# Regrouping the attention matmuls in a fused attention and bilinear kernel

## The chip, the cores and the metric

The kernel runs on one core of one Trainium2 chip. Its metric is the device time of one execution in microseconds (us), and lower is better. The core has a matmul engine (PE, with its weight loads shown as PEld), a vector engine (DVE), a scalar engine (ACT), a third engine for elementwise work (POOL), and a queue engine (SP) that issues nearly all transfers between memory and the core.

## The reference

Attention inside chunks of 64 tokens, for 8 batches of 576 tokens and 8 heads of size 64, is followed by a bilinear feed-forward layer over all 4608 tokens:

```python
q_c = q.reshape(B, H, nc, chunk, D)          # the same for k and v; chunk = 64
scores = scale * np.matmul(q_c, k_c.transpose(0, 1, 2, 4, 3))
scores = scores - np.max(scores, axis=-1, keepdims=True)
attn = np.exp(scores)
attn = attn / (np.sum(attn, axis=-1, keepdims=True) + 1e-09)
out = np.matmul(attn, v_c)                   # back to (B, H, S, D)

x = out.transpose(0, 2, 1, 3).reshape(B * S, H * D)     # 4608 x 512
a = x @ w_a                                  # 512 x 1536
b = x @ w_b
y = a * b @ w_out                            # 1536 x 512
```

## The kernel before

**Tiling.** The tokens are cut into 18 units of 256 for the attention, and 9 blocks of 512 (two units each) for the feed-forward part. All instruction orders are written out by hand: nothing reorders instructions within an engine, and each engine runs its own list in order, held up only by what it waits for.

**One unit of attention** has these steps:
- `load` brings q, k and v from memory in float32 on SP's queue. Eight staging buffers (`st`) are shared by all loads.
- `cast` makes bfloat16 copies on POOL (`q_raw`, `k_raw`, `v_raw`; for q and k of unit 0 on DVE).
- q and k are transposed into `qkt`. Units 0 to 4 use PE (`transpose_pe`, L231) with copies out of PSUM by DVE and ACT (L240). From unit 5 on, SP issues two DMA transposes per unit (`transpose_dma`, L245), which wait for the casts.
- `scores` are 64 small matmuls of 64x64 (L265) into two PSUM banks, and then two exponentials on ACT (L276), one for each bank, giving E.
- `sums` multiply E by ones on PE, four 64x64 matmuls of 512 columns (L292), into two banks; ACT takes the logarithm (L302).
- `inverse` is an exponential of minus that logarithm on ACT (L311), either for both halves at once or for one half (`cl`).
- `values` are 64 small matmuls of E with v (L325) into two banks; DVE multiplies each bank by the inverse sums and writes `xT` (L334).

All these matmuls but the transposes use PE as four tiles of 64x64; all others use it whole (128x128).

**The feed-forward part** takes three forms. Block 0 uses whole steps (`ab_step`, L388: a pair of four matmuls for wb and wa; ACT copies one bank out, L396; DVE multiplies, L397). Block 1 does the same in halves of 256 tokens, `h(1)` being one pair for a strip `ft` of 128 columns; there are 24, ft 0 to 11 for each half. From block 2 on, one level of Strassen-like sums is used: `Group` does seven products (`p1` to `p7`, L438) with ACT copies (L449, L456) and DVE sums and products (L476, L477, L488). The output of block 0 is made by `out_part` (L642, three parts of four matmuls for each 128 tokens), and that of later blocks by `OutGroup` (L574) in 14 parts `n0` to `n6`, two each, which a list `chunks` deals out over the Groups of the next block. These parts need sums that POOL makes (`combine_ab` L518, `combine_wo` L164): n3 needs the last `combine_wo`, and n5 the sum `so4`.

**The order around the change.** At the start, PE does transposes of unit 0, q transposes of unit 1, scores of 0, k transposes of 1, sums of 0, two warm-up matmuls, scores of 1, values of 0. In the second half of block 1, attention of units 4 and 5 is strewn between the pairs ft 7 to 11 and the outputs of block 0, with each step of attention on its own. In block 2, `attention` says after which product each step runs; from block 3 on, the scores of the next unit follow the values of the one before directly, through `scores_beside`, with one exponential at once and the other after `p5`.

**PSUM.** There are eight banks: one each in `psum_a`, `psum_c`, `psum_o`, `psum_q`, two buffers in `psum_t` taken in turn, and two pools in the list `psum_b`, which each call of `bank(psum_b)` turns round by one. `bank()` without a pool takes the next of the list `spread`:

```python
        if pool is None:
            pool = spread[0]
            spread.append(spread.pop(0))
        if pool is psum_b:
            pool = psum_b[0]
            psum_b.append(psum_b.pop(0))
```

In block 1 `spread` is `[psum_t, psum_b]`, so that each step of attention takes one bank of either kind. A matmul into a bank waits until the last reader of its earlier content is done.

Of the kernel before, what the change touches and what calls it, by code (L numbers as in the profile page):

```python
# [16 lines left out]
def kernel(  # L17
# [49 lines left out]
    psum_b = [psum_b0, psum_b1]  # L67
    psum_c = ctx.enter_context(tc.tile_pool(name="psumc", bufs=1, space=PSUM))
    psum_o = ctx.enter_context(tc.tile_pool(name="psumo", bufs=1, space=PSUM))
# [27 lines left out]
    def keep_warm(n):  # L97

        t = bank()
        for _ in range(n):  # L100
            nc.tensor.matmul(t, warm_in[:, :128], warm_in, start=True, stop=True)
# [85 lines left out]
    def load(U, names="qkv"):  # L187

        for n in names if U < NU else "":
            src = {"q": q, "k": k, "v": v}[n]  # L190
            if U < PE_UNITS and n != "v":
                st = st_pool.tile([128, H, 2, D], FP32, name="st")
                for r, b, s, m in pieces(U):
                    nc.sync.dma_start(
                        out=st[r // 2:(r + m) // 2].rearrange("p h i d -> p h (i d)"),
                        in_=src[b, :, s:s + m, :].rearrange("h (p i) d -> p h (i d)", i=2),
                    )
                staged[n, U] = st.rearrange("p h i d -> p i h d")
            else:
                staged[n, U] = st_pool.tile([128, 2, H, D], FP32, name="st")  # L200
                load_natural(staged[n, U], src, U)
# [16 lines left out]
    def transpose_pe(U, names="qk"):  # L218
        if U not in qkt:
            qkt[U] = qkt_pool.tile([128, 2, 2, NKT, 128], BF16, name="qkt")  # L220
        for n in names:
            w = "qk".index(n)
            src = raw.pop((n, U))
            t = [bank() for _ in range(2 if U < 2 else 1)]
            tp = [
                t[i % len(t)].bitcast(BF16).rearrange("c (i m p) -> c i m p", i=2, m=NKT)[:, i]
                for i in range(2)
            ]
            for i in range(2):
                for m in range(NKT):  # L230
                    nc.tensor.transpose(  # L231
                        tp[i][:, m, :],
                        src[:, i, 2 * m:2 * m + 2, :].rearrange("p j d -> p (j d)"),
                        identity,
                    )
            dst = qkt[U][:, w].rearrange("c g m (p i) -> c i m g p", i=2)
            for i in range(2):
                on_dve = i == 0 if U == 0 else w == 0 or U == 1
                cp = nc.vector.tensor_copy if on_dve else nc.scalar.copy
                cp(out=dst[:, i], in_=tp[i].rearrange("c m (g p) -> c m g p", g=2))  # L240
# [13 lines left out]

    late = []

    def scores(U, pools=(None, None)):
        t = qkt.pop(U)
        E_of[U] = sm_pool.tile([128, 2, NKT, 2, 64], BF16, name="E")
        sc = [bank(p).rearrange("p (m g s) -> p m g s", m=NKT, g=2) for p in pools]  # L260
        for m in range(NKT):
            for g in range(2):
                for j in range(2):
                    for cl in range(2):
                        nc.tensor.matmul(  # L265
                            sc[j][cl * 64:cl * 64 + 64, m, g, :],
                            t[j * 64:j * 64 + 64, 1, g, m, cl * 64:cl * 64 + 64],
                            t[j * 64:j * 64 + 64, 0, g, m, cl * 64:cl * 64 + 64],
                            start=m == 0 and g == 0,
                            stop=True,  # L270
                            skip_group_check=True,
                        )
        E = E_of[U]
        for j in range(2):
            late.append(
                lambda j=j: nc.scalar.activation(  # L276
                    out=E[:, j], in_=sc[j], func=AF.Exp, scale=scale
                )
            )
        exps(1 if pools[0] else 2)  # L280

    def exps(n=2):
        while late and n:
            late.pop(0)()
            n -= 1

    def sums(U, halves=None):
        E = E_of[U]
        sm = [bank() for _ in range(2)]
        for cl in range(2):  # L290
            for j in range(2):
                nc.tensor.matmul(  # L292
                    sm[cl][j * 64:j * 64 + 64, :],
                    ones[cl * 64:cl * 64 + 64, :],
                    E[cl * 64:cl * 64 + 64, j].rearrange("p m g s -> p (m g s)"),
                    start=True,
                    stop=True,
                )
        ln_of[U] = sm_pool.tile([128, 2, NKT, 128], FP32, name="ln")
        rs_of[U] = ln_of[U]  # L300
        for cl in range(2):
            nc.scalar.activation(  # L302
                out=ln_of[U][:, cl].rearrange("p m n -> p (m n)"), in_=sm[cl], func=AF.Ln
            )
            if halves:
                inverse(U, cl)

    def inverse(U, cl=None):

        for c in [slice(0, 2)] if cl is None else [cl]:  # L310
            nc.scalar.activation(  # L311
                out=rs_of[U][:, c], in_=ln_of[U][:, c], func=AF.Exp, scale=-1.0
            )
# [39 lines left out]
    def bring(U, before_v=()):  # L353

        if U >= NU:
            return
        cast(U, "qk")
        load(U + 1, "q" if U < 8 else "qkv")
        transpose_dma(U)
        for args in before_v:  # L360
            cast(*args)
        bring_v(U)

    def bring_v(U):
        cast(U, "v")
        if U < 8:
            load(U + 1, "kv")

    ab_tiles = {}
# [268 lines left out]
    def out_part(K, tg, part, pool):  # L638
        if part == 0:
            out_ps[K, tg] = bank(pool)  # L640
        for ft in range(4 * part, 4 * part + 4):
            nc.tensor.matmul(  # L642
                out_ps[K, tg],
                ab_tiles[K][:, ft, tg * 128:tg * 128 + 128],
                wo_sb[:, ft],
                start=(ft == 0),
                stop=(ft == NFT - 1),
            )
        if part == 2:
            out_tile(K, tg, out_ps.pop((K, tg)))  # L650

    with tc.manual_schedule(
# [25 lines left out]
        cast_ab(1)  # L678
        cast_ab(2)
        cast_ab(3)  # L680
        transpose_pe(1, "q")
        scores(0)
        transpose_pe(1, "k")
        sums(0, halves=None)
        keep_warm(2)
        scores(1)
        inverse(0)
        values(0)
# [66 lines left out]
        def h(n=1):  # L755
            for _ in range(n):
                half(*halves.pop(0))

        def normalize(U):
            sums(U)  # L760
            inverse(U)

        def out_0(tg):
            for p in range(3):
                out_part(0, tg, p, psum_b)
# [19 lines left out]
        scores(4)  # L785
        out_0(1)
        h(1)
        normalize(4)
        h(1)
        scores(5)  # L790
        cast(7, "q")
        h(1)
        combine_ab(1, 0, 1)
        cast(7, "k")
        load(8, "q")
# [2 lines left out]
        combine_ab(1, 2, 1)  # L798
        bring_v(7)
        values(4)  # L800
        h(1)
        spread[:] = [psum_q, psum_o]
        out_part(0, 2, 0, psum_b)
        normalize(5)
        out_part(0, 2, 1, psum_b)
        out_part(0, 2, 2, psum_b)
        spread[:] = [psum_t]
        values(5)
        h(1)
# [10 lines left out]
        def at(K, i, n, f, u):  # L820
            if u < NU:
                attention.setdefault((K, i, n), []).append(lambda: f(u))

        def scores_beside(pool):
            return lambda u: scores(u, (pool, psum_b[0]))

        for K in range(2, NBLK):
            U = 2 * K + 2
            if K == 2:
                at(K, 0, 0, lambda u: combine_x(2, (2, 3)), U)  # L830
                at(K, 0, 0, scores, U)
                at(K, 0, 1, sums, U)
            else:
                attention[K, 0, 0] = [lambda K=K: combine_x(K, (2,))]
                attention[K, 0, 1] = [lambda K=K: combine_x(K, (3,))]
                at(K, 0, 0, sums, U)
            at(K, 1, 0, inverse, U)
            at(K, 2, 1, values, U)
            at(K, 2, 1, scores_beside(psum_o), U + 1)
            at(K, 3, 0, sums, U + 1)  # L840
            at(K, 3, 1, inverse, U + 1)
            at(K, 4, 1, values, U + 1)
            if K == 2:
                at(K, 5, 1, scores, U + 2)
            else:
                at(K, 4, 1, scores_beside(psum_q), U + 2)
            at(K, 5, 0, lambda u: combine_x(u // 2, (0,)), U + 1)
            at(K, 5, 1, lambda u: combine_x(u // 2, (1,)), U + 1)

        def attend(K, i, n):  # L850
# [2 lines left out]

        last = None
        chunks = {
            2: (1, 1, 1, 1, 1, 2, 1, 2, 1, 1, 2, 1),
            4: (1, 1, 1, 1, 2, 1, 1, 2, 2, 0, 1, 1),
            NBLK - 1: (1,) * 12,
        }
# [8 lines left out]
        for K in range(2, NBLK):  # L868
            for i in range(NWP):
# [16 lines left out]
                now = Group(K, i)  # L886
# [72 lines left out]
```

The softmax here doesn't subtract the row's maximum and nothing guards it: scores larger than these inputs give would overflow.

## Time and profile before

| | |
|---|---|
| median of 7 runs | 304.65 us (303.8 to 305.18) |
| the profiled execution | 303.8 us, of which the span of its instructions is 302.0 |
| PE | busy 289.0 us, 96% of the span |
| DVE, ACT, POOL | busy 208.0, 196.2 and 193.6 us |
| first feed-forward matmul (L388) | 18.61 us |
| first product of block 2 (L438) | 79.46 us |
| first product of block 3 | 110.94 us |
| granted PE clock | full throughout |

All times within the span are counted from its start. A row of the timeline gives start, duration, engine, line, operation, output and inputs, shape and count. A row of the waits gives the total, the number and the longest of them, for one line of an engine and what it waited for. The chain of waits is followed back from the last instruction to what released each step.

### The profile page before, as it was taken

To read this page: it belongs to the slowest core of one execution; us is meant where nothing else is said; L and a number is where in the kernel's file an instruction comes from. 1 tells how busy PE (TensorE), PEld (TensorE's weight loads), DVE (VectorE), ACT (ScalarE), POOL (GpSimd) and SP (SyncE) were. 2 spreads that over 40 slices of the span, in tenths; PEclk is the share of its full clock that TensorE was granted. 3 is DMA by queue.
4 is the path that set the end of the run, shared out by engine and by line. 5 is a ranking of instruction groups with operands and counts; after the bars stand their busy time and mean duration, and the time that the engine had idled before them with its cause. 6 is when DMAs were issued, how large, how long until landed. Compare 5 with 4: busy or idle time off the path is not lost.

```text
span 302.0 us, 8543 instructions
## 1 busy us (share of the span) xinstructions
PE 289.0 (96%) x3497; PEld 231.1 (77%) x3499; DVE 208.0 (69%) x339; ACT 196.2 (65%) x354; POOL 193.6 (64%) x180
## 2 busy tenths in 40 slices
PE   2889999999999999999999999999999999999995
PEld 1434467866587888888888888888888888888884
DVE  3446665865886686769677966796679667965773
ACT  2553567447586668776877687768776876566522
POOL 0666758994999897728880888178817901790660
PEclk9999999999999999999999999999999999999999
DMA  7999999998999999799969585958621001100025
GB/s 229 302 377 285 276 328 361 226 219 191 218 265 227 230 218 255 176 206 226 289 121 216 165 202 112 224 176 192 138 75 72 2 2 69 73 0 3 0 92 188
DMA packets 143079, 54.56 MB, mean 181 GB/s; under 512 B 120256, under 2 KB 137152, under 8 KB 143040
## 3 DMA queue, kind: packets, MB, share of 16 engines
q1 hardware_dynamic: 142896, 53.88, 71.4%
q8 instruction: 27, 0.44, 0.6%
q10 hardware_dynamic: 144, 0.13, 0.1%
q14 instruction: 12, 0.10, 0.1%
HBM read 37.75 MB, written 9.44 MB: 156 GB/s over the span
## 4 chain that ended last, share of the span: by engine, by line
PE 74%; POOL 9%; DMA 8%; SPq 3%; ACT 2%; DVE 2%; issue 2%; POOLq 0%; DVEq 0%; ACTq 0%
PE pb L438 18%; PE pc L438 12%; PE po L574 11%; PE pa L438 11%; PE pq L574 9%; DMA st<-in_q_dram 3%; PE pb L388 3%; DMA st<-in_moe_w_out_dram 3%; SPq L182 2%; POOL so L518 2%; POOL wot L164 2%; DMA st<-in_v_dram 2%; PE pc L388 1%; PE po L388 1%; PE pt L292 1%
## 5 line engine op out<-in xcount | busy, mean ns | idle before, releaser
L518 POOL TENSOR_TENSOR so<-ab_sb 128x512 f16<-128x512 f16 x23 | 27.6, 1198 | 65.9 <-DVE ab_sb L488 65.9
L438 PEld LDWEIGHTS <-t 128*128 128x128 f16 x504 | 48.3, 98 | 8.5 <-issue 1.8
L438 PE MATMUL pb<-s,wa 128*128 128x256 f16 x336 | 50.6, 273 | 0.0
L438 PE MATMUL pa<-xT,wb 128*128 128x256 f16 x336 | 50.4, 273 | 0.0
L476 DVE TENSOR_TENSOR c_sb<-pc,v_sb 128x512 f32<-128x512 f32 x42 | 28.9, 687 | 26.2 <-ACT v_sb L449 26.2
L574 PEld LDWEIGHTS <-ab_sb 128*128 128x128 f16 x384 | 37.6, 98 | 4.7 <-issue 0.4
L438 PEld LDWEIGHTS <-wb 128*128 128x128 f16 x336 | 32.9, 98 | 4.0
L438 PEld LDWEIGHTS <-wa 128*128 128x128 f16 x336 | 31.7, 98 | 4.3 <-issue 0.2
L449 ACT COPY u_sb<-pb 128x512 f32<-128x512 f32 x42 | 24.7, 587 | 15.8 <-PE pb L438 15.6
L488 DVE SCALAR_TENSOR_TENSOR ab_sb<-pc,c_sb 128x512 f16<-128x512 f32 x42 | 29.0, 689 | 7.8 <-PE pc L438 6.3
L488 DVE SCALAR_TENSOR_TENSOR ab_sb<-pb,b_sb 128x512 f16<-128x512 f32 x42 | 29.0, 689 | 6.8 <-PE pb L438 5.9
L574 PEld LDWEIGHTS <-so 128*128 128x128 f16 x288 | 28.1, 98 | 3.6 <-issue 0.3
L456 ACT COPY pb<-pa 128x512 f32<-128x512 f32 x42 | 24.0, 572 | 10.4 <-PE pa L438 10.1
L449 ACT COPY b_sb<-pa 128x512 f32<-128x512 f32 x42 | 25.0, 595 | 8.1 <-PE pa L438 6.9
L477 DVE TENSOR_TENSOR pc<-pc,u_sb 128x512 f32<-128x512 f32 x42 | 28.9, 688 | 0.0
L518 POOL TENSOR_TENSOR so<-so,ab_sb 128x512 f16<-128x512 f16 x23 | 27.0, 1174 | 1.7
L449 ACT COPY v_sb<-pb 128x512 f32<-128x512 f32 x42 | 24.6, 586 | 4.7 <-PE pb L438 3.9
L518 POOL TENSOR_TENSOR ab_sb<-ab_sb 128x512 f16<-128x512 f16 x23 | 26.7, 1162 | 0.0
L518 POOL TENSOR_TENSOR so<-ab_sb,so 128x512 f16<-128x512 f16 x23 | 26.1, 1161 | 0.0
L438 PE MATMUL pb<-s,t 128*128 128x256 f16 x168 | 25.3, 273 | 0.0
L438 PE MATMUL pc<-xT,t 128*128 128x256 f16 x168 | 25.2, 272 | 0.1
L438 PE MATMUL pc<-s,t 128*128 128x256 f16 x168 | 25.2, 273 | 0.0
(133 smaller groups left out, 561.1 us busy)
## 6 DMA issues: line engine op xcount, KB each, us to landing
out_dram<-o_sb SPq DMA_DIRECT2D x34, 256.0 KB, 2.4
st<-in_v_dram SPq DMA_DIRECT2D x32, 256.0 KB, 4.8
st<-in_q_dram SPq DMA_DIRECT2D x25, 256.0 KB, 4.1
st<-in_k_dram SPq DMA_DIRECT2D x25, 256.0 KB, 4.3
st<-in_moe_w_b_dram SPq DMA_DIRECT2D x6, 512.0 KB, 7.2
st<-in_moe_w_a_dram SPq DMA_DIRECT2D x6, 512.0 KB, 6.6
st<-in_moe_w_out_dram SPq DMA_DIRECT2D x6, 512.0 KB, 7.2
st<-in_q_dram SPq DMA_DIRECT2D x3, 512.0 KB, 5.8
```

What stands on the lines that cost most here:

```text
L164: nc.gpsimd.tensor_tensor(out=o, in0=x0, in1=x1, op=op)
L182: nc.sync.dma_start(out=st[p:p + n, g], in_=src[b, :, s:s + n, :].rearrange("h p d -> p h d"))
L292: nc.tensor.matmul(sm[cl][j * 64:j * 64 + 64, :], ones[cl * 64:cl * 64 + 64, :], E[cl * 64:cl * 64 + 64, j].rearrange("p m g s -> p (m g s)"),
L388: nc.tensor.matmul(ps[n], w_ab[n, i][:, kt, o:o + 128], xT[:, kt, c0:c1], start=(kt == 0), stop=(kt == NKT - 1),)
L438: nc.tensor.matmul(t[:, h * 256:h * 256 + 256], w[:, kt, h * 128:h * 128 + 128], x[:, kt], start=start and h == 0 and kt == 0, stop=h == 1 ...
L449: nc.scalar.copy(out=t, in_=src)
L456: nc.scalar.copy(out=self.B, in_=self.A)
L476: nc.vector.tensor_tensor(out=self.c, in0=self.C, in1=self.v, op=ADD)
L477: nc.vector.tensor_tensor(out=self.C, in0=self.C, in1=self.u, op=ADD)
L488: nc.vector.scalar_tensor_tensor(out=self.dst[:, :, c0:c0 + 256], in0=t.rearrange("p (h n) -> p h n", h=2), scalar=AB_SCALE, in1=o.rearran ...
L518: (eng or nc.gpsimd).tensor_tensor(out=o, in0=x0, in1=x1, op=op)
L574: nc.tensor.matmul(t[:, c0:c0 + 256], a[:, kt, th * 128:th * 128 + 128], w[:, kt], start=n in (0, 4) and first and kt == 0, stop=last and ...
```

## The change

The change moves steps of attention on PE, and what belongs to them on the other engines.

- At the start, scores of unit 0 come ahead of both transposes of unit 1, and one of the two warm-up matmuls behind the sums is left out. `sums(0)` loses an argument that said what the default says.
- In block 1, sums of 4 are followed directly by scores of 5, whose exponentials are put off past the next pair; values of 4 are followed directly by sums of 5. The inverse of 4 is cut into two halves, one on either side of a pair. sums(5) take banks from `psum_t` and `psum_b` instead of `psum_q` and `psum_o`, so `psum_b` turns once more. The three parts of `out_part(0, 2)` are no longer split by sums of 5.
- In block 2, scores of 8 follow values of 7 directly, beside `psum_q`, as in the later blocks. The list `chunks` of block 2 takes three output parts in one place, so that the last part that uses `psum_q` is done ahead of them.
- `load` of unit 9 is split: k and v of unit 9 are loaded behind the DMA transposes of unit 8, instead of ahead of them.
- `scores` gets a parameter `now` for the number of exponentials issued at once; `normalize` is taken out.

```diff
-    def scores(U, pools=(None, None)):
+    def scores(U, pools=(None, None), now=2):
...
-        exps(1 if pools[0] else 2)
+        exps(now)
...
-        load(U + 1, "q" if U < 8 else "qkv")
+        load(U + 1, "q" if U < 9 else "qkv")
...
     def bring_v(U):
         cast(U, "v")
-        if U < 8:
+        if U < 9:
             load(U + 1, "kv")
...
         cast_ab(3)
-        transpose_pe(1, "q")
         scores(0)
-        transpose_pe(1, "k")
-        sums(0, halves=None)
-        keep_warm(2)
+        transpose_pe(1)
+        sums(0)
+        keep_warm(1)
         scores(1)
...
-        def normalize(U):
-            sums(U)
-            inverse(U)
...
         scores(4)
         out_0(1)
         h(1)
-        normalize(4)
+        sums(4)
+        scores(5, now=0)
         h(1)
-        scores(5)
+        exps()
+        inverse(4, 0)
         cast(7, "q")
         h(1)
+        inverse(4, 1)
         combine_ab(1, 0, 1)
...
         values(4)
+        sums(5)
         h(1)
-        spread[:] = [psum_q, psum_o]
-        out_part(0, 2, 0, psum_b)
-        normalize(5)
-        out_part(0, 2, 1, psum_b)
-        out_part(0, 2, 2, psum_b)
+        inverse(5)
+        for p in range(3):
+            out_part(0, 2, p, psum_b)
         spread[:] = [psum_t]
         values(5)
         h(1)
...
         def scores_beside(pool):
-            return lambda u: scores(u, (pool, psum_b[0]))
+            return lambda u: scores(u, (pool, psum_b[0]), 1)
...
-            if K == 2:
-                at(K, 5, 1, scores, U + 2)
-            else:
-                at(K, 4, 1, scores_beside(psum_q), U + 2)
+            at(K, 4, 1, scores_beside(psum_q), U + 2)
...
-            2: (1, 1, 1, 1, 1, 2, 1, 2, 1, 1, 2, 1),
+            2: (1, 1, 1, 1, 1, 2, 1, 2, 3, 0, 1, 1),
```

## The prediction

> **What bounds the kernel now.** I read the waits of the matmul engine (PE) first, since PE is busy 96% of the span; columns are total us, times, longest us.
>
> ```profile
> PE pt L231 <- DVE q_raw L213: 5.4, 1, 5.4
> ...
> PE pb L388 <- DVE xT L334: 0.8, 1, 0.8
> ...
> PE pt L265 <- DMA qkt<-k_raw: 0.2, 1, 0.2
> ```
>
> After the start-up PE hardly waits: the end is PE's own stream from 18.61 us on, plus any new wait. Idle time under about 0.17 us hides behind the modelled ends of pipelined matmuls, so the starts in PE's timeline are the better ruler (start us, us, what):
>
> ```profile
> 68.04 0.60 PE L388 MATMUL pq<-xT,wb 128*128 128x256 f16 x4
> 68.48 0.60 PE L388 MATMUL po<-xT,wa 128*128 128x256 f16 x4
> 69.00 0.40 PE L292 MATMUL pt<-E,ones 64*64 64x512 bf16 x2
> 69.01 0.40 PE L292 MATMUL pb<-E,ones 64*64 64x512 bf16 x2
> 69.35 0.61 PE L388 MATMUL pa<-xT,wb 128*128 128x256 f16 x4
> ```
>
> Four 128*128 matmuls of 256 columns advance PE by 0.436 us; ahead of the 64*64 group the step is 0.52, so entering costs 0.09. The last sums start at 69.01, 512 columns stream in 0.216 (L642: 12 in 2.60), and L388 resumes at 69.35: leaving costs 0.12. Each separate 64*64 block costs **0.21 us** of switching.
>
> Three places tie PE to work on its own clock. PE's wa group at 34.33 follows a cast that ends at 34.27, 0.15 us later than PE's stream alone would have it:
>
> ```profile
> 33.23 1.04 POOL L120 CAST wa<-st 128x1024 f16<-128x1024 f32 x1
> 34.33 1.04 PE L388 MATMUL pc<-xT,wa 128*128 128x512 f16 x4
> ```
>
> Scores(6) at 81.09 come 0.23 late, for a DMA transpose. And the chain of waits runs through DMA and POOL up to 95.78 and enters PE inside an L574 group, where PE loses 0.25:
>
> ```profile
> 94.63 1.16 POOL wo L164
> 95.78 0.04 issue
> 95.82 0.38 PE pq L574 x2
> ```
>
> PE time gained ahead of such an anchor is lost at it; time lost ahead of it is refunded up to that slack.
>
> **What the Trainium skill says.** "TensorEngine Tiling (Array Packing)", Key Properties: changing the tiling mode drains the engine; the trace agrees, 0.21 us in and out. "TensorE: Matmul & The Clock Gate", Part 2, Step-by-step: only weight loads are pulled ahead, matmuls stay in program order, so one that waits holds all behind it; the trace agrees at 81.09. Same page, Part 1: PE runs at half clock until a window of about 3.4 us was busy; the trace agrees, four transposes advance PE by 0.40 us at 8.78, eight by 0.45 at 30.69.
>
> **Start-up.** scores(0) can start when ACT's copy from pc ends, 8.72. The k transposes of unit 1 wait for a POOL cast that ends at 10.28, before and after. Scores(0), 0.6 us when cold, no longer fill the gap behind the q transposes; E is there by about 10.5 instead of 11.5, so sums(0) at 11.30 need not wait. DVE's q copies come 0.6 later and push its k copies from 12.33 to about 12.63; scores(1), at 13.01 behind two warm matmuls before, can start near 12.7. ACT's chain to xT gains 0.3. If the warm matmul taken out delays the full clock, 0.3 to 0.6 is lost instead. A gain ends at the 34.33 anchor, a loss is refunded 0.15. I take 0 (0 to +0.45).
>
> **Block 1, saved:** sums(4)+scores(5) and values(4)+sums(5) make two blocks out of four: −0.42.
>
> **Block 1, new wait 1, the transpose.** Scores(5) were at 70.33; now they follow sums(4) at 69.00+0.22 = 69.22. Their k half comes by DMA:
>
> ```profile
> 67.17 1.25 SPq L245 DMA_TRANSPOSE qkt<-k_raw  x1
> ...
> DMA to landing us min/median/max: 2.9/2.9/2.9
> ```
>
> It lands at 70.1, and nothing ahead of it on SP or POOL changes. PE stands from 69.22 to 70.16: **+0.94**, with all L388 work behind it. Scores take 0.37 with the switch, so the L388 pair of ft 8 starts at 70.53, ft 9 at 71.41, values(4) 72.37, sums(5) 72.63, ft 10 72.97 to 73.84. ACT, with its steps of 0.25 to 0.54 from its timeline: Ln(4) 69.48, copy of ft 8 71.16, exp(5) 71.41 to 72.49 (just in time for sums(5)), inverse(4,0) 72.39, copy of ft 9 72.93 to 73.30, inverse(4,1) to 73.81.
>
> **Block 1, new wait 2, the bank.** sums(5) now take a psum_b bank, which shifts the rotation by one. out_part(0,2) used to reuse the bank of scores(5); it now reuses that of values(4), which DVE's second xT product must have read. DVE before:
>
> ```profile
> 73.19 0.42 DVE L397 SCALAR_TENSOR_TENSOR ab_sb<-po,u_sb 128x256 f16<-128x256 f32 x1 [0.49 <-ACT u_sb L396]
> 73.53 0.68 DVE L334 TENSOR_TENSOR xT<-pt,ln 128x512 f16<-128x512 f32 x1
> 74.13 0.68 DVE L334 TENSOR_TENSOR xT<-pb,ln 128x512 f16<-128x512 f32 x1
> ```
>
> The products stand behind ft 9's L397, which waits for ACT's copy (73.30): 73.33, 73.67, 74.27 to 74.95. PE is ready at 73.85 and goes on at 75.00: **+1.15**. Bounds: 0.4 (ACT runs ahead) to 1.5. Behind it stand out_part(0,2), values(5) and p1 of block 2.
>
> Balance: out_part(0,2) at 75.00 against 72.95, with the 0.43 of sums(5) already done: +1.62, which is 0.94+1.15−0.42 but for rounding. The wait of 0.23 at scores(6) goes, and the 0.25 at 95.82: **+1.14**. POOL is not delayed in turn: it reaches block 1's sums at 77.98 to 88.54, eight us or more after DVE made them.
>
> **Block 2.** values(7)+scores(8): −0.21. The three out parts now in a row ahead of p3 give DVE 1.3 us, so the late p4 at 102.49 (0.11) and p7 at 105.00 (0.07) go: −0.18. New waits: n5 needs POOL's so4, done 102.06, and PE comes later than that (0.16 if PE were on time). scores(8) need pq read by ACT's o_sb copy, done some 1.3 us earlier by my count; K>2 runs this order without a wait on PE. scores(8) move from 109.67 to 104.9+1.1, and their transposes move ahead of four loads: they were issued at 101.78 and 104.58, now at about 97.4 and 100.1, landing near 103; cover 3 us. The four loads of unit 9's k and v move behind, so the cast of k, at 103.01 before, waits until about 107 (4.3 us to landing), and POOL's sums for block 2 slip 3 us; their s2, done 117.24, is needed by PE at 120.55. Cover 3.3 us, some 2 left with POOL's pause before 114.75. If it is gone, up to 1. I take 0. Removing `normalize` and the new default `now` issue nothing.
>
> **Sum:** 1.62−0.23−0.25−0.21−0.18 = **+0.75 us** against the profiled execution, 303.8 (span 302.0). That run equals the lowest of the seven; the median is 304.65. Added to the median: **305.4**.
>
> **The rivals.**
> A. Not slower: POOL hides it. The median run is 0.85 longer than the profiled one; if that is later DMA and POOL work, the anchor at 95.8 stands 0.85 later and refunds that much more: 0.75−0.85 = −0.1, 304.55. It decides once POOL's last wo product, 95.78 in this profile, ends after 96.5. For: the chain runs through POOL there. Against: the profile doesn't show where other runs lose time.
> B. Faster: the new waits don't form (the transpose lands by 69.2, ACT runs ahead). Then both anchors eat the 0.42, and −0.39 to −0.2 remains; only if the anchors come earlier too, −0.8, 303.85. Against: 70.1 is a landing in the trace, and the bank's reader is fixed by program order.
> C. Slower: a late cast or transpose of unit 8 or 9, or a cold start, adds 0.5 to 1.2: 306.2. Against: the covers of 2 to 3 us.
>
> **Chances.** Forecast 0.48, A 0.26, B 0.14, C 0.12. 0.2% is 0.61 us, about what a measurement of this kernel can tell from no change. The forecast's own range is 304.7 to 306.0; 0.40 of it lies over the bound and 0.08 within; A gives 0.25 within and 0.01 over; B 0.11 under and 0.03 within; C 0.12 over. Faster 0.11, same 0.36, slower 0.53. Range 304.0 to 306.6: it leaves out half of B and the tail of C.
>
> **What would show it.** Right: L265 of unit 5 starting at about 70.2 behind a DMA wait; a PE wait of about 1 us at L642 for DVE's xT near 75; no PE wait at scores(6) or in the L574 group near 96; first L388 near 18.3 with the wait at 34.33 grown. Wrong: L642 going on before 73.5, the wo anchor still holding PE, PE waiting for so near 120, or the wait at 34.33 gone.

## The result, and the profile after

The changed kernel takes **306.35 us** in the median of 14 runs (304.68 to 307.31). The kernel before, run beside it, takes 304.15 us (35 runs, 303.41 to 305.57). The ratio is **1.0065, with a 95% interval of 1.0050 to 1.0081**: 2.0 us slower by the ratio, 2.2 by the medians. A few executions fall into a slower state (two of g_loads below, one each of e_block2 and b_t5); they are left out of every ratio, but not of the medians and ranges. The profiled execution of the changed kernel took 306.35 us with a span of 304.6, so the two profiles stand 2.55 us (time) and 2.6 us (span) apart. That is more than the medians do, because the profiled execution before was one of the faster ones of its kernel.

PE's waits after (line of the engine, what it waited for; total us, times, longest us):

```profile
PE pt L265 <- DMA qkt<-k_raw: 1.6, 1, 1.6
PE pb L642 <- DVE xT L334: 1.0, 1, 1.0
...
PE pq L574 <- POOL so L518: 0.5, 1, 0.5
PE pb L388 <- DVE xT L334: 0.5, 1, 0.5
...
PE pc L438 <- DVE ab_sb L488: 0.2, 1, 0.2
```

Before, the first of these was 0.2 (for unit 6, not unit 5), and the second, third and last were not on the list. The three new ones and the larger first one add 1.4+1.0+0.5+0.2 = 3.1 us by this view; waits of the start-up stand apart. PE's timeline shows where they lie, and what the starts say (start us, us, what, and in brackets the wait that the trace assigns):

```profile
68.23 0.60 PE L388 MATMUL po<-xT,wa 128*128 128x256 f16 x4
68.76 0.40 PE L292 MATMUL pt<-E,ones 64*64 64x512 bf16 x2
68.76 0.40 PE L292 MATMUL pb<-E,ones 64*64 64x512 bf16 x2
70.79 0.22 PE L265 MATMUL pt<-qkt 64*64 64x64 bf16 x2 [1.62 <-DMA qkt<-k_raw]
...
71.16 0.61 PE L388 MATMUL pa<-xT,wb 128*128 128x256 f16 x4
...
74.06 0.60 PE L388 MATMUL pc<-xT,wa 128*128 128x256 f16 x4
75.66 2.75 PE L642 MATMUL pb<-wo,ab_sb 128*128 128x512 f16 x12 [1.00 <-DVE xT L334]
...
81.72 0.60 PE L438 MATMUL pa<-xT,wb 128*128 128x256 f16 x4
...
104.50 1.05 PE L574 MATMUL pq<-wo,so 128*128 128x256 f16 x8 [0.53 <-POOL so L518]
...
113.08 0.60 PE L438 MATMUL pc<-s,t 128*128 128x256 f16 x4 [0.21 <-DVE ab_sb L488]
```

There are four steps in the starts. Sums(4) are over at 68.76 + 0.22 = 68.98, and scores(5) begin at 70.79: 1.81 us without a matmul. Each L388 half-strip group of four takes 0.44, so out_part(0,2) was due at 74.50 and begins at 75.66: 1.16. The starts say 0.69 at 104.50 and 0.37 at 113.08 where the brackets say 0.53 and 0.21, because a gap of some 0.16 hides behind the modelled ends.

The balance of starts, changed kernel minus kernel before, with before in brackets where the prediction did not print it:

| place | after − before, us | what happened on the way |
|---|---|---|
| sums(4) (69.00) | −0.24 | start-up: first L388 at 18.43 for 18.61, wa group at 34.06 for 34.33 |
| first product of block 2 (79.46) | +2.26 | +1.81 and +1.16 of waits, −0.42 of switches, and rounding |
| scores(6) (81.09) | +2.03 | the 0.23 of wait before is gone |
| sums of unit 7 (96.57) | +1.86 | the wait for the last wo product is gone (0.17 of its 0.25) |
| a product early in block 3 (112.90) | +2.58 | +0.69 and +0.37 of waits, −0.34 of switch and late p4, p7 |
| last products (297.87) | +2.56 | nothing changes from 113 us on |

The chain of waits, which before ran through POOL into an L574 group at 95.82, now runs through a load, a cast and POOL's sums into another L574 group, and on through DVE:

```profile
93.59 6.36 DMA st<-in_v_dram
...
100.07 1.04 POOL v_raw L213
101.11 1.91 POOL so L518 x2
103.02 0.28 issue
103.30 1.15 POOL so L518
104.45 0.05 issue
104.50 1.05 PE pq L574 x8
...
110.51 0.04 DVE ab_sb L488
110.54 0.57 issue
111.12 1.31 DVE s L418
```

### The profile page after: what moved, and what is told of

Same layout as the page of the kernel before. It is cut to its first block, busy times and chain, and to the rows that moved or that the text cites. A ratio compares the mean times of both kernels' runs of the same rounds, so it can differ in the third digit from the quotient of the medians.

```text
span 304.6 us, 8544 instructions
## 1 busy us (share of the span) xinstructions
PE 288.4 (95%) x3497; PEld 231.2 (76%) x3498; DVE 211.0 (69%) x339; ACT 196.2 (64%) x355; POOL 193.2 (63%) x180
## 3 DMA queue, kind: packets, MB, share of 16 engines
q1 hardware_dynamic: 142896, 53.88, 70.4%
## 4 chain that ended last, share of the span: by engine, by line
PE 62%; DMA 16%; POOL 10%; SPq 6%; issue 2%; DVE 2%; POOLq 0%; DVEq 0%
PE pb L438 17%; PE pc L438 11%; PE pa L438 11%; PE po L574 11%; PE pq L574 9%; DMA st<-in_moe_w_a_dram 5%; DMA st<-in_v_dram 4%; SPq L182 3%; POOL wot L164 3%; DMA st<-in_k_dram 3%; DMA st<-in_moe_w_out_dram 3%; DMA st<-in_moe_w_b_dram 2%; POOL so L518 2%; POOL v_raw L213 2%; SPq L194 1%
## 5 line engine op out<-in xcount | busy, mean ns | idle before, releaser
L438 PEld LDWEIGHTS <-t 128*128 128x128 f16 x504 | 48.3, 98 | 8.8 <-issue 2.3
L438 PE MATMUL pb<-s,wa 128*128 128x256 f16 x336 | 50.5, 273 | 0.0
L438 PE MATMUL pa<-xT,wb 128*128 128x256 f16 x336 | 50.4, 273 | 0.0
L574 PEld LDWEIGHTS <-ab_sb 128*128 128x128 f16 x384 | 37.5, 98 | 4.8 <-issue 0.4
L438 PEld LDWEIGHTS <-wb 128*128 128x128 f16 x336 | 32.9, 98 | 4.0
L438 PEld LDWEIGHTS <-wa 128*128 128x128 f16 x336 | 31.8, 98 | 4.2 <-issue 0.2
L574 PEld LDWEIGHTS <-so 128*128 128x128 f16 x288 | 28.0, 98 | 4.2 <-POOL so L518 0.8
L438 PE MATMUL pc<-s,t 128*128 128x256 f16 x168 | 25.2, 273 | 0.2 <-DVE ab_sb L488 0.2
L438 PE MATMUL pb<-s,t 128*128 128x256 f16 x168 | 25.3, 273 | 0.0
L438 PE MATMUL pc<-xT,t 128*128 128x256 f16 x168 | 25.2, 272 | 0.1
```

What stands on the lines that cost most here:

```text
L438: nc.tensor.matmul(t[:, h * 256:h * 256 + 256], w[:, kt, h * 128:h * 128 + 128], x[:, kt], start=start and h == 0 and kt == 0, stop=h == 1 ...
L574: nc.tensor.matmul(t[:, c0:c0 + 256], a[:, kt, th * 128:th * 128 + 128], w[:, kt], start=n in (0, 4) and first and kt == 0, stop=last and ...
```

## The experiments

The theory: block 1 carries the loss, through two waits that have separate causes (unit 5's k transpose at L265, and the psum_b bank at L642). The rivals: the cold start at the beginning, or the moved loads of unit 9 with what they delay in block 2, carry it. All ratios are to the kernel before, run beside each on the same chip, with medians of 303.98 to 304.26; 0.003 is 0.9 us.

### Each part of the change alone

**e_start**: the start-up part in the kernel before.

```diff
-        transpose_pe(1, "q")
         scores(0)
-        transpose_pe(1, "k")
-        sums(0, halves=None)
-        keep_warm(2)
+        transpose_pe(1)
+        sums(0)
+        keep_warm(1)
```

> The kernel before with the start-up part of the change alone (scores of unit 0 ahead of unit 1's transposes, one warm-up matmul less). Theory (two new waits in block 1 make the loss): first L388 at about 18.4 instead of 18.6, and the gain ends at the cast that PE waits for near 34, so the time is that of before within 0.2 us. Rival (the start is colder and loses): 0.6 us or more slower than before, with the first L388 at 18.9 or later.

Measured: 304.45 us, ratio 1.0011 (0.9991 to 1.0032). First L388 at 18.40, wa group at 34.11, so 0.2 us is gained by then. Its profile loses that and more in block 1, where the order is the old one, but the transposes were late in this execution. Its wait line:

```profile
PE pt L265 <- DMA qkt<-k_raw: 1.4, 2, 0.9
```

That line (0.9 of it for unit 5, 0.5 for unit 6) is the first sign that the transposes' time is not fixed.

The cold start is real, but it does not carry the loss. In the kernels with the new start-up, 51 of 127 executions have a mean granted PE clock (as a share of full speed) of 0.994 or less; in those with the old one, 13 of 258. Two profiles of the first kind (g_loads and f_bank, below) show where: the clock is at 0.50 for about 3.4 us from 15.8 us on. The warm-up matmuls in it, of the change and then of g_loads:

```profile
16.23 1.69 PE L101 MATMUL po<-warm_in 128*128 128x512 bf16 x7
```

```profile
16.17 3.15 PE L101 MATMUL po<-warm_in 128*128 128x512 bf16 x7
```

The first L388 then comes at 19.13 in g_loads, for 18.43 in the change. Yet in e_start the 8 executions with the lower clock have a median of 304.45, the other 14 one of 304.37; in the change it is 306.04 for 6 and 306.37 for 8. So executions at the full clock are as slow.

**e_block1**: the block 1 part alone (the edits of the diff from `sums(4)` to the three `out_part(0, 2, p)`, and the parameter `now`).

```diff
-        normalize(4)
+        sums(4)
+        scores(5, now=0)
...
         values(4)
+        sums(5)
         h(1)
-        spread[:] = [psum_q, psum_o]
-        out_part(0, 2, 0, psum_b)
-        normalize(5)
...
+        inverse(5)
+        for p in range(3):
+            out_part(0, 2, p, psum_b)
```

> The kernel before with the block 1 part alone (sums of 4 with scores of 5, values of 4 with sums of 5, the halves of the inverse, the shifted bank). Theory: PE waits 1 to 1.8 us for unit 5's transpose at L265 and 1.0 to 1.2 us for DVE's xT at L642, the waits at scores(6) and at n3 near 96 go, and the time is 1.0 to 2.0 us over before. Rival (the moved loads and POOL's late sums in block 2 make the loss): under 0.6 us over before.

Measured: 306.11 us (9 runs), ratio 1.0046 (1.0014 to 1.0078). Both waits are there:

```profile
PE pb L642 <- DVE xT L334: 1.0, 1, 1.0
PE pt L265 <- DMA qkt<-k_raw: 0.9, 1, 0.9
```

**e_block2**: the block 2 part with the split load alone.

```diff
-        load(U + 1, "q" if U < 8 else "qkv")
+        load(U + 1, "q" if U < 9 else "qkv")
...
-            if K == 2:
-                at(K, 5, 1, scores, U + 2)
-            else:
-                at(K, 4, 1, scores_beside(psum_q), U + 2)
+            at(K, 4, 1, scores_beside(psum_q), U + 2)
...
-            2: (1, 1, 1, 1, 1, 2, 1, 2, 1, 1, 2, 1),
+            2: (1, 1, 1, 1, 1, 2, 1, 2, 3, 0, 1, 1),
```

> The kernel before with the block 2 part alone (values of 7 with scores of 8, the output parts dealt out anew, unit 9's k and v loaded behind unit 8's transposes). Theory: 0.4 us gained by one switch less and DVE's two waits, against 0 to 0.7 us of PE waiting for POOL's so4 at n5 and for DVE in the next group: -0.4 to +0.4 us against before. Rival (this part makes the loss): 1 us or more slower.

Measured: 304.38 us, ratio 1.0005 (0.9987 to 1.0023). The three point estimates add up to 0.0062, near the 0.0065 of the whole, with block 1 at 0.0046 of it. Two lines of its waits matter:

```profile
PE pt L265 <- DMA qkt<-k_raw: 1.0, 1, 1.0
PE pc L438 <- DVE ab_sb L488: 0.3, 1, 0.3
```

The first is again in a part of the kernel that this edit leaves alone. The second is the wait of the changed kernel at 113.08, so it belongs to block 2's part. There is no wait for `so` here: the one at 104.50 is not a fixed cost of the edit.

**g_loads**: the changed kernel with unit 9's k and v loaded ahead of unit 8's transposes, as before.

```diff
-        load(U + 1, "q" if U < 9 else "qkv")
+        load(U + 1, "q" if U < 8 else "qkv")
...
-        if U < 9:
+        if U < 8:
```

> The changed kernel with the loads of unit 9's k and v back ahead of unit 8's transposes. Theory: the late product p7 of block 2's last group (0.3 to 0.4 us, DVE's x sums slowed while POOL's sums run late beside them) goes, but scores of unit 8 now wait for their transpose for 0 to 1.2 us; the time is that of the changed kernel, within 0.6 us. Rival (the moved loads make a good part of the loss): 0.8 us or more faster than the changed kernel.

Measured: 308.2 us (11 runs, 304.96 to 310.9), ratio 1.0091 (1.0060 to 1.0122). That is a miss for the theory, which had it level with the change, and the rival falls: taking the moved loads back does not bring the time down. That the loads are a help is not shown. Nine of the 11 executions have a clock of 0.994 or less, against 6 of 14 of the change, and the two at the full clock took 305.63 and 306.53, inside the change's range. PE now waits for unit 8's k transpose, which lands at 106.51; the wait for `ab_sb` at L438 is gone:

```profile
PE pq L265 <- DMA qkt<-k_raw: 0.3, 1, 0.3
```

This profile is of the shortest execution (span 303.2), so it does not show where the long ones lose up to 6 us. That stays open.

### Each merge of block 1 alone

**g_sums5**: only values(4) with sums(5), in the kernel before.

```diff
         values(4)
+        sums(5)
         h(1)
-        spread[:] = [psum_q, psum_o]
-        out_part(0, 2, 0, psum_b)
-        normalize(5)
-        out_part(0, 2, 1, psum_b)
-        out_part(0, 2, 2, psum_b)
+        inverse(5)
+        for p in range(3):
+            out_part(0, 2, p, psum_b)
```

> The kernel before with the sums of unit 5 moved directly behind the values of unit 4, on the psum_t and psum_b banks, and nothing else; scores of unit 5 stay where they were. Theory (the shifted bank costs by itself): PE waits 1.3 to 1.8 us at L642 for DVE's xT, 0.2 of switching is saved, up to 0.5 is refunded at scores(6) and n3: 0.8 to 1.4 us over before. Rival (the transpose makes the whole loss): within 0.3 us of before.

Measured: 305.14 us, ratio 1.0033 (1.0017 to 1.0049): slower by itself. The bank wait comes with this merge, with next to nothing of the transpose wait:

```profile
PE pb L642 <- DVE xT L334: 0.5, 1, 0.5
...
PE pt L265 <- DMA qkt<-k_raw: 0.2, 1, 0.2
```

By the starts the bank wait is 0.70 here (1.3 to 1.8 had been expected), and PE also stands 0.26 and 0.48 inside sums(5) for exponentials, which this kernel issues later than the change does.

**g_scores5**: only sums(4) with scores(5), and the inverse of 4 in halves, in the kernel before.

```diff
-        normalize(4)
+        sums(4)
+        scores(5, now=0)
         h(1)
-        scores(5)
+        exps()
+        inverse(4, 0)
...
         h(1)
+        inverse(4, 1)
```

> The kernel before with the scores of unit 5 moved directly behind the sums of unit 4 (exponentials and the two halves of the inverse as in the changed kernel), and nothing else; the sums of unit 5 stay on psum_q and psum_o. Theory (the transpose costs by itself): PE waits for it 0.9 to 2 us at L265, of which the kernel before has 0 to 1 already, 0.2 of switching is saved: 0.3 to 0.9 us over before. Rival (the bank makes the whole loss): within 0.2 us of before.

Measured: 304.3 us, ratio 1.0002 (0.9981 to 1.0022). No loss can be told here, which is a miss for the theory that this merge alone costs. The wait is there, small, since the transpose was issued at 67.08 and landed at 69.84 in this execution:

```profile
PE pt L265 <- DMA qkt<-k_raw: 0.4, 1, 0.4
```

The starts give 0.60 (69.07 + 0.22 = 69.29 to 69.89), of which the saved block of 0.21 gives some back. The kernel before is no zero to measure from either: with its order, PE waits 0.9 and 1.0 for this transpose in the profiles of e_start and e_block2.

### The waits taken away

**f_t5**: the changed kernel with unit 5's transposes ahead of the load of unit 6's q.

```diff
+        if U == 5:
+            transpose_dma(U)
         load(U + 1, "q" if U < 9 else "qkv")
-        transpose_dma(U)
+        if U != 5:
+            transpose_dma(U)
```

> The changed kernel with unit 5's two DMA transposes issued ahead of the load of unit 6's q instead of behind it. Theory: the transposes land before 69 us, PE's wait of 1.6 us at L265 goes and the one of 1.0 us at L642 stays; part of the gain is lost again at scores(6) and n3, so 0.8 to 1.6 us faster than the changed kernel, that is 0.4 to 1.4 us over before. Rival (the wait for the transpose was only cover for another one that ends as late, such as the exponentials): no more than 0.3 us faster than the changed kernel.

Measured: 304.61 us, ratio 1.0023 (1.0008 to 1.0039), which lies below the changed kernel's interval. The k transpose is issued at 65.56 and landed at 68.78; scores(5) start at 68.99 with no DMA wait at L265. The bank wait stays (the edit moves the later lines by 3):

```profile
PE pb L645 <- DVE xT L334: 1.0, 1, 1.0
```

So the bank wait does not hang on the transpose. By the points the transpose wait is worth about 1.3 us (0.0065 − 0.0023 of 304); from the two intervals I estimate 0.6 to 2.0.

**f_bank**: the changed kernel with ft 11's pair ahead of out_part(0,2), the transposes left where they are.

```diff
         sums(5)
-        h(1)
+        h(2)
         inverse(5)
         for p in range(3):
             out_part(0, 2, p, psum_b)
         spread[:] = [psum_t]
         values(5)
-        h(1)
```

> The changed kernel with the last pair of unit 8's projections in block 1 (feature tile 11) ahead of the first output product, so that VectorE has the second xT product behind it by then; unit 5's transposes stay where the change has them. Theory (two waits, each with its own cause): the bank wait of 1.16 us at L642 falls to about 0.2, the transpose wait at L265 stays at 0.9 to 1.8, and the kernel is about 0.9 us faster than the changed one, at a ratio near 1.003 to the kernel before. Rival (the transpose wait alone carries the loss, and what is taken out at L642 comes back at the next step): within 0.3 us of the changed kernel.

Measured: 305.06 us (303.59 to 308.04, 22 runs), ratio 1.0034 (1.0010 to 1.0058): 0.9 us below the change by the points, as expected, though the two intervals overlap. Its profiled execution has no wait at L642, and a much larger one at L265:

```profile
72.83 0.22 PE L265 MATMUL pt<-qkt 64*64 64x64 bf16 x2 [2.82 <-DMA qkt<-k_raw]
...
74.23 1.06 PE L388 MATMUL pq<-xT,wb 128*128 128x256 f16 x4
75.09 1.06 PE L388 MATMUL po<-xT,wa 128*128 128x256 f16 x4
```

This was one of its longest executions (307.5, mean clock 0.989). Behind the wait the granted clock is at 0.50 again, from 73.9 to 77.3, and four matmuls advance PE by 0.86 instead of 0.44. Four of the 22 executions have a clock of 0.988 or 0.989; they took 307.50 to 308.04.

**f_both**: both repairs.

```diff
+        if U == 5:
+            transpose_dma(U)
         load(U + 1, "q" if U < 9 else "qkv")
...
         sums(5)
-        h(1)
+        h(2)
...
```

> The changed kernel with unit 5's transposes ahead of the load of unit 6's q, and with the last L388 pair of block 1 (ft 11) moved ahead of out_part(0,2). Theory (PE waits at L642 for DVE's products because the bank rotation was shifted): the pair's 0.87 us of PE work cover the wait, which falls from 1.0 us to 0.3 or less; 0.3 to 0.9 us faster than with the transposes moved alone, so -0.5 to +0.4 us against before. Rival (DVE itself is late, whatever stands in front): the wait moves to the next reader of xT or of a psum_t bank and the time is that of the version with the transposes moved alone, within 0.2 us.

Measured: 304.4 us (14 runs, 302.44 to 306.5), ratio 0.9996 (0.9969 to 1.0022): level with the kernel before, and below the changed kernel's interval. Its profile has the lowest span of all, 301.7. What is left of the waits:

```profile
PE pq L577 <- POOL so L521: 0.3, 1, 0.3
PE pc L441 <- DVE ab_sb L491: 0.3, 1, 0.3
...
PE pb L645 <- DVE xT L334: 0.2, 1, 0.2
```

Taking both waits away takes the whole loss away, which puts it on these two. How it divides between them is not settled: f_t5 and f_bank give 1.3 and 0.9 by the points, while g_scores5, built up from the kernel before, gives the transpose wait nothing that can be told. The move of ft 11 was not tried in the kernel before, so what it would gain there is not known.

### Is there a version that beats both?

**b_t5**: the kernel before with the early transposes of unit 5.

```diff
+        if U == 5:
+            transpose_dma(U)
         load(U + 1, "q" if U < 8 else "qkv")
-        transpose_dma(U)
+        if U != 5:
+            transpose_dma(U)
```

> The kernel before with one edit: unit 5's two transposes issued ahead of the load of unit 6's q, as in the repair of the changed kernel. Theory (the landing of these transposes varies and the kernel before also waits for them in some executions, up to 1.2 us): no excess ahead of scores(5), 0.2 to 0.6 us faster than before. Rival (the kernel before has its cover: the landing is in time in nearly all executions): within 0.2 us of before.

Measured: 304.28 us (22 runs), ratio 0.9989 (0.9968 to 1.0011): no difference that can be told. Unit 5's transpose lands at 69.38, ahead of its use, but unit 6's is now late, between 78 and 90 us:

```profile
PE pt L265 <- DMA qkt<-k_raw: 0.9, 1, 0.9
```

So what is gained in block 1 can be given back one unit later; one profile does not say how often it is.

**f_best**: start-up and block 1 as in f_both, with block 2 and its loads as in the kernel before.

```diff
-        load(U + 1, "q" if U < 9 else "qkv")
+        load(U + 1, "q" if U < 8 else "qkv")
...
-            at(K, 4, 1, scores_beside(psum_q), U + 2)
+            if K == 2:
+                at(K, 5, 1, scores, U + 2)
+            else:
+                at(K, 4, 1, scores_beside(psum_q), U + 2)
...
-            2: (1, 1, 1, 1, 1, 2, 1, 2, 3, 0, 1, 1),
+            2: (1, 1, 1, 1, 1, 2, 1, 2, 1, 1, 2, 1),
```

> Start-up and block 1 as the change has them, with both repairs (unit 5's transposes ahead of the load of unit 6's q, feature tile 11 ahead of the first output product), and block 2 with its loads as before. Theory (the change's switches in block 1 are worth 0.42 us once neither wait stands in their place, and the late cast of unit 9's k and the wait that it leads to at L438 stay away): 0.3 to 1.0 us faster than before. Rival (what the repairs leave open is filled at a later wait): level with before, as with both repairs and the change's block 2.

Measured: 303.9 us (22 runs, 303.25 to 306.52), ratio 0.9986 (0.9966 to 1.0005): 2.4 us faster than the change, and not to be told from the kernel before. The waits at L577 and at L441 for `ab_sb` are gone. The forecast gain of 0.3 to 1.0 us over the kernel before can be neither shown nor excluded. Two transposes were late in its profiled execution, a long one (305.75), unit 5's (issued at 67.40 even ahead of the load) and unit 6's:

```profile
PE pt L265 <- DMA qkt<-k_raw: 2.5, 2, 1.3
```

## Why the prediction was right, and where it was off

The sign and the range held: slower by over 0.2%, and 306.35 lies within 304.0 to 306.6. The sum did not: +0.75 us was forecast, and the ratio says +2.0, the medians +2.2, the two profiles +2.56. The forecast's own range, 304.7 to 306.0, was missed; the number lies nearest to rival C's 306.2, 0.25 under the upper end of the range, and that it fell inside is luck. So is part of its nearness: the sum was added to a median of 304.65, and with more runs that is 304.15. Between the profiles the 1.81 that is missing (2.56 − 0.75; that a wait has the same length is chance) is 0.87 at the transpose, 0.69 and 0.37 at two waits in block 2, less 0.24 at the start; the rest of 0.12 is in the refunds and the savings. Of C's mechanism, something late for unit 8 or 9 is part of it, and the cold start is not.

- **Switches, −0.42 and −0.39: right.** Block 1's balance closes to 0.05 us with −0.42 in it, and block 2's with −0.34 for the switch and the late p4 and p7. As "TensorEngine Tiling (Array Packing)", Key Properties, says that a mode switch drains the engine, fewer blocks do save; the trace agrees with 0.21 us a block.
- **New wait 2, the bank, +1.15: right**, 1.16 by the starts, with its releaser as named. DVE's products stand behind L397 and its wait for ACT:

```profile
73.98 0.42 DVE L397 SCALAR_TENSOR_TENSOR ab_sb<-po,u_sb 128x256 f16<-128x256 f32 x1 [0.91 <-ACT u_sb L396]
74.32 0.68 DVE L334 TENSOR_TENSOR xT<-pt,ln 128x512 f16<-128x512 f32 x1
74.92 0.68 DVE L334 TENSOR_TENSOR xT<-pb,ln 128x512 f16<-128x512 f32 x1
```

  They end at 75.60, and out_part(0,2) starts at 75.66. The whole row of products stands 0.65 us later than the prediction put it (75.00), since PE came from the transposes that much later: the size of the wait was kept, not its place.
- **New wait 1, the transpose, +0.94: the term that was mis-sized.** It is 1.81: PE came 0.24 earlier than before, so that the gain of the start-up was lost here, and the landing was 0.63 later than forecast. The mechanism was right; the step that failed is "it lands at 70.1, and nothing ahead of it on SP or POOL changes". The order on the queues doesn't change, but the time does, from execution to execution. The transpose's row, of the changed kernel and then of f_bank, with the trace's answer on its landing:

```profile
67.85 1.24 SPq L245 DMA_TRANSPOSE qkt<-k_raw  x1
...
DMA to landing us min/median/max: 2.9/2.9/2.9
```

```profile
69.77 1.24 SPq L245 DMA_TRANSPOSE qkt<-k_raw  x1
...
DMA to landing us min/median/max: 3.0/3.0/3.0
```

  The transfer is as steady as I took it, 2.8 to 3.0 us over the nine profiled executions that have the old queue order up to there (the kernel before, the change, e_start, e_block1, e_block2, g_sums5, g_scores5, g_loads, f_bank). Its issue is not: 66.49 to 69.77 in the nine, and 67.17 in the one that I read, the third earliest. In the change SP falls behind step by step as it issues the loads ahead: against the kernel before it is 0.43 late at v of unit 5 (58.21), 0.53 at q of unit 6 (62.70) and 0.66 at the q transpose (66.40). In f_bank POOL is late as well: a load of w_out landed at 52.79 instead of 50.80, and POOL's casts followed it. What makes these loads slower is not shown. The median landing of the nine, about 70.4, makes this wait an estimated 1.4 (70.4 − 68.98); f_t5 prices it at 1.3.
- **The refunds, −0.23 and −0.25: right**, 0.23 and 0.17. Neither wait is left in the profile after, as the prediction's signs had it.
- **Start-up, 0 (0 to +0.45): a small gain went through**, 0.24. I took the wait at 34.33 for an anchor; the wa cast ended at 34.00 in this execution (it starts at 32.96) and let PE pass. With that, one sign of my being wrong came true: the wait at 34.33 was gone, down to 0.06, where I had it grown. Alone (e_start) the gain can't be told from nothing. The clause on the warm matmul taken out has something to it, though not as a delay of the full clock: the clock falls a second time, in two profiles for certain and by the means in up to 51 of 127 executions. In g_loads that costs 0.70 us at the first L388, more than the 0.3 to 0.6 named. Which edit of the start-up does it was not tested. The table ahead has the granted clock full throughout; the transposes at 8.78, at about half pace, show that it can't be so at the very start.
- **so4, 0: wrong in this execution, by 0.69.** The prediction held so4's time, 102.06, fixed as well. The cast of v(8) waited for its load, and POOL's sums behind it slipped:

```profile
100.07 1.04 POOL L213 CAST v_raw<-st 128x1024 bf16<-128x1024 f32 x1 [2.07 <-DMA st<-in_v_dram]
101.07 3.38 POOL L518 TENSOR_TENSOR so<-ab_sb,so 128x512 f16<-128x512 f16 x3
```

  That load took 6.36 us here and 4.9 before. The wait is not in e_block2 or f_t5 and is 0.45 in f_both, so it comes and goes; why the load was slow is not shown.
- **The moved loads, 0: the cover named for `s2` held, and another one was overlooked.** PE does not wait near 120, as forecast. But the late cast of k(9) (108.76 for 103.01; forecast about 107) pushes POOL's sums beside a DVE sum on which a product of L438 hangs. The POOL rows after, then the DVE row:

```profile
108.76 1.04 POOL L213 CAST k_raw<-st 128x1024 bf16<-128x1024 f32 x1 [3.33 <-DMA st<-in_k_dram]
109.76 1.15 POOL L518 TENSOR_TENSOR so<-ab_sb 128x512 f16<-128x512 f16 x1
110.99 1.15 POOL L518 TENSOR_TENSOR so<-so,ab_sb 128x512 f16<-128x512 f16 x1
112.10 1.34 POOL L518 TENSOR_TENSOR ab_sb<-ab_sb 128x512 f16<-128x512 f16 x1
```

```profile
111.12 1.31 DVE L418 TENSOR_TENSOR s<-xT 128x512 f16<-128x512 f16 x1
```

  The same DVE sum took 0.41 us before, at 108.42. PE waits 0.37 at 113.08 for the product behind it. The wait is 0.42 in e_block2, 0.28 in f_t5, 0.43 in f_both, and absent in g_loads and f_best, which have the old loads. So it comes with the moved loads. It is rival C's kind of mishap, though C had put it down to a late cast that PE waits for directly.
- **Rival A falls:** the wait near 96 did vanish, and no refund larger than 0.17 came. **Rival B falls** in the medians; half of it can happen: in g_loads' profiled execution the transpose landed at 69.35 and scores(5) hardly stood, helped by a PE that came 0.84 later than in the change (sums(4) at 69.60), while the bank wait formed there too, 1.20.

What stays open: why f_both and f_best, which keep the saved switches and lose both waits, do not come out 0.5 us or more ahead of the kernel before. Their profiles show later transposes and sums waited for, which fits, but one profile each does not price these waits in the medians. The clock may have a part in f_both: its 7 executions at 0.994 or less have a median of 304.65, the other 7 one of 303.69; but f_best shows no such difference (303.83 for 7, 303.98 for 15).

## What to carry to other kernels

Merging small blocks to save mode switches moves each consumer nearer to its producer; price the saving (0.21 us a block) against the earliest time at which every operand and every bank is free, and move the producer's issue first. The issue of a DMA in one profile is one draw: here the latest of nine came 2.6 us behind the one that was read, so a smaller margin is no cover. Its duration held while the queue order stayed (2.8 to 3.0); moved ahead of the load, the k transpose took 3.2 or 3.3 and the q one up to 5.4. A rotation of banks that one more tenant turns changes who must have read the bank: 1.16 us here, beside 1.81 for the late operand.

## What the runs showed of the hardware that I had not expected

A DVE sum with both inputs in SBUF was held up by POOL's sum: L418 took 1.31 us in the changed kernel and 0.41 us before. "SBUF — State Buffer", section "SBUF: two separate sides", says that such a DVE operation and a GpSimd operation that reads SBUF share a port pair as an exclusive lock, held for the whole instruction. The trace agrees: POOL's sum ran from 110.99 to 112.14, DVE's started at 111.12 and ended at 112.43, 0.29 us after POOL's had ended. In e_block2 it took 1.35 us beside POOL's sum from 109.18 to 110.34; there, in f_t5 and in f_both it ended 0.27 to 0.28 us after POOL's. Where DVE came first (before, at 108.42), it kept its 0.41, and POOL's cast at 108.47 took 1.26 instead of the 1.03 and 1.04 of the two casts before it.

The issue of the same DMA transpose, behind an unchanged queue order, moved by 3.3 us between executions, while its time from issue to landing was 2.9 in the kernel before and 3.0 in the latest one.

The granted clock fell to 0.50 for about 3.4 us three times in two profiles: from 15.8 us in g_loads and from 15.9 in f_bank, both with the new start-up, and from 73.9 in f_bank, after PE had waited 2.8 for the transpose. After the wait of 1.6 in the changed kernel it stayed full. No run varies the length of a wait by itself, so the cause is not shown.
